# Loading the first batch's queries and keys in whole rows, and turning them one head at a time

## The chip, the cores and the metric

The program runs on one core of a Trainium2 chip. The metric is device time in microseconds (us) of one execution. TensorE (PE) does the matrix products, VectorE (DVE), ScalarE (ACT) and GpSimd (POOL) the elementwise work, and SyncE (SP) issues every transfer between memory and the core. Sixteen DMA engines carry the transfers out.

## The reference, cut to what matters

Windowed attention over 4 batches, 8 heads, 576 tokens and a head size of 64, then a two-layer MLP, then a gated MLP. All inputs are float32 or wider.

```
scores = q @ k.T / sqrt(64)          # heads 0-3: window of 32; heads 4-7: every 4th of the last 128
attn   = softmax(where(mask, scores, -1e9))
x  = attn @ v                        # as 2304 tokens x 512
x2 = leaky_relu(x @ w_in) @ w_out    # 512 -> 2048 -> 512
y  = ((x2 @ w1) * (x2 @ w2)) @ w3 @ w_out2
```

## The kernel before, in words

**Heads.** Two heads make a pair, so a pair of a batch fills the 128 rows of the PE array with 2 x 64. A batch has four pairs: two with the dilated mask, which come first, and two with the plain one. `seq` is the order of the pairs, and the number m in `load_qk(m)` and `transpose_qk(m)` counts q and k through it. So m = 0 to 7 is the first batch (`m < 2 * HP`).

**Loading q and k** (`load_qk`, issue at L244). For a pair with c = 8 (dilated) or 6 (plain), each of n = 576 / c partitions holds c consecutive tokens: 72 or 96 partitions. In the tile, the token comes before the head, so that one token's two heads lie side by side:

```
t = win_p.tile([P, 8, 2, D], F32, tag="win", ...)
nc.sync.dma_start(t[:n, :c, j, :], rows(src, o + j * S * D, [[c * D, n], [D, c], [1, D]]))
```

There is one transfer for each head j. It writes runs of 64 floats (256 bytes), 576 of them.

**Turning q and k round** (`transpose_qk`, L306). For each of c token positions, one PE transpose takes n x 128 (both heads) to 128 x n in a PSUM bank; DVE copies half a tile at a time to `qT` (L309, with the scale) or `kT` (L311). The scores of a pair (L328) follow, then mask and maximum on DVE (L336, L338), exponentials on ACT (L341), the turn of the probabilities (L371, L373), and the values (L389, L420, L422).

**Weights.** The inputs of both MLPs are 64-bit floats. A `conv.fetch()` issues one raw weight tile of 512 KB (L127 for w_in, L124 for w_out, in turn); a `conv.step()` converts one tile with POOL (L103), ACT (L143, L145, L107) and DVE (L146, L147, L108) and fetches the next. There are 32 tiles for the first MLP. Eight can be fetched before one is converted.

**Order.** SP's instructions keep the order in which the program writes them; the other engines are ordered by a planner that estimates times and takes what is ready, in the program's order of importance. The order at the start is one string. A digit loads q and k of a pair of the first batch, a letter a to d loads values (`load_v`, L282), M builds the masks, F fetches a weight tile, X starts the attention, A does two of its steps, C converts a weight tile:

```
for x in "0aM1bFF2cFF3dFFFFXAAAAAAAAAAAACCCCCCCC":
```

The weight tiles that these F fetch are called F0 to F7 here, and the four pairs by their digits. After this start the hidden layer (L112 to L114 into `ps_h`) and its projection (`ps_x`) run on PE, with the attention of later batches woven in.

Of the kernel before, what the change touches and what calls it, by code (L numbers as in the profile page):

```python
# [8 lines left out]
F32 = mybir.dt.float32  # L9
# [19 lines left out]
def tile_window_attention_two_mlps(  # L29
# [14 lines left out]
    nc = tc.nc  # L44
    P = 128
    B, H, S, D = q.shape
# [5 lines left out]
    NF = F1 // P  # L52
# [12 lines left out]
    HP = H // 2  # L65


    def pool(name, side):
        es = ExitStack()
        return es, es.enter_context(  # L70
            tc.tile_pool(name=name, bufs=1, side=side, reuse_waits="tile")
        )
# [3 lines left out]
    win_es, win_p = pool("win", "left")  # L76
# [17 lines left out]
    ident = const.tile([P, P], F32, name="ident")  # L94
# [24 lines left out]
    def rows(t, off, dims):  # L119
        return bass.AP(t.tensor, t.offset + off, dims)  # L120
# [67 lines left out]
    win, wout, w12, wo2, wp = {}, {}, {}, {}, {}  # L188
# [37 lines left out]
    def pair(pi):  # L226
        b, h0 = divmod(pi, HP)
        return b, 2 * h0, 2 * h0 < H // 2

    def load_qk(m):  # L230
        if m >= 2 * NPAIR:
            return
        pi, nm = seq[m // 2], "qk"[m % 2]
        b, h0, plain = pair(pi)
        c = 6 if plain else 8
        n = S // c
        if m < 2 * HP:
            t = win_p.tile([P, 8, 2, D], F32, tag="win", name=f"{nm}{pi}", bufs=NF)
        else:
            t = att.tile([P, 8, 2, D], F32, tag="nat", name=f"{nm}{pi}", bufs=2)  # L240
        src = q if nm == "q" else k
        o = (b * H + h0) * S * D
        for j in range(2):
            nc.sync.dma_start(  # L244
                t[:n, :c, j, :], rows(src, o + j * S * D, [[c * D, n], [D, c], [1, D]])
            )
        nat_t[nm, pi] = t


# [8 lines left out]
    def load_v(m):  # L258


        if m >= 4 * B:
            return
        b, plain, r = m // 4, m % 4 >= 2, m % 2
        o = (b * H + (0 if plain else H // 2)) * S * D
        bl = R_BLOCKS[r]
        tiles = []
        if m >= 4:
            t = att.tile([KB, NQ, H // 2, D], F32, tag="v", name=f"v{m}", bufs=2)
            tiles = [t[:, i] for i in range(len(bl))]
        else:  # L270
            for i0 in range(0, len(bl), 4):
                t = win_p.tile([KB, 4, H // 2, D], F32, tag="win", name=f"v{m}_{i0}", bufs=NF)
                tiles += [t[:, i] for i in range(min(4, len(bl) - i0))]
        for i, t in zip(bl, tiles):
            k0 = s0 = first_key(i, plain)
            while s0 < k0 + KB:
                if plain:
                    s1, token, st = k0 + KB, s0, D
                else:
                    s1 = min(k0 + KB, (s0 // SR + 1) * SR)  # L280
                    token, st = s0 % SR * DILATION + s0 // SR, DILATION * D
                nc.sync.dma_start(  # L282
                    t[s0 - k0 : s1 - k0], rows(v, o + token * D, [[st, s1 - s0], [S * D, H // 2], [1, D]])
                )
                s0 = s1
        v_t[m] = tiles

    def transpose_qk(m):

        if m >= 2 * NPAIR:  # L290
            return
        pi, nm = seq[m // 2], "qk"[m % 2]
        plain = pair(pi)[2]
        c = 6 if plain else 8
        n = S // c
        t = nat_t.pop((nm, pi))
        dst = att.tile([P, S], F32, tag=nm + "T", name=f"{nm}T{pi}", bufs=2)
        if plain:
            to = dst.rearrange("d (p g c) -> d g c p", g=2, p=n)
        else:  # L300
            to = dst.rearrange("d (c p g) -> d g c p", g=2, p=n)
        for g in range(2):
            ps = (bank if m < 2 * HP else side_bank)(f"ps_{nm}T{pi}_{g}")
            for c1 in range(c // 2):
                src = t[:n, g * (c // 2) + c1].rearrange("p j d -> p (j d)")
                nc.tensor.transpose(ps[:, c1 * n : (c1 + 1) * n], src, ident[:n, :n])  # L306
            src = ps[:, : S // 2].rearrange("d (c p) -> d c p", p=n)
            if nm == "q":
                nc.vector.tensor_scalar(to[:, g], src, SCALE, None, op0=ALU.mult)  # L309
            else:  # L310
                nc.vector.tensor_copy(to[:, g], src)  # L311
        qk_t[nm, pi] = dst
# [116 lines left out]
    def attention(n0, n1):  # L429

        for n in range(n0, n1):
            if n == N_EARLY:
                for m in range(NA, NA + 2):
                    load_qk(m)
                load_v(4)
                for m in range(NA, n + 4):
                    transpose_qk(m)
                    load_qk(m + 2)
                load_v(5)
            transpose_p(n)  # L440
            normalize(n + 1)
            yield
            if n % 8 != 3:
                scores(n + 2)
                yield
            if n >= N_EARLY or n + 4 < NA:
                transpose_qk(n + 4)
            if n >= N_EARLY:
                load_qk(n + 6)
            yield  # L450
            if n % 8 == 3:
                scores(n + 2)
                yield
            values(n)
            if n >= NA:
                m = n // NA * 4
                if n % NA in (2, 3):
                    load_v(m + n % NA)
                elif n % NA in (5, 7):
                    load_v(m + 4 + (n % NA == 7))  # L460
            yield
# [178 lines left out]
    with ExitStack():  # L640
# [5 lines left out]
        def build_masks():  # L646


            def band(m, shift):
                for j in range(2):  # L650
                    mj = m[j * QB : (j + 1) * QB]
                    for base, sign in ((shift, 1), (WINDOW - 1 - shift, -1)):
                        nc.gpsimd.affine_select(
                            out=mj, in_=mj, compare_op=ALU.is_ge, fill=NEG, base=base,
                            pattern=[[-sign, KB]], channel_multiplier=sign,
                        )

            shifts = [i * QB - first_key(i, False) for i in range(S // QB)]
            band(mask_d[:, 0], shifts[0])
            band(mask_d[:, 1], WINDOW)  # L660
            nc.vector.tensor_copy(mask_p[:, 0], mask_d[:, 0])
            for m in (mask_d[:, 2:], mask_p[:, 1:]):
                nc.vector.tensor_copy(m, mask_d[:, 1:2].to_broadcast(list(m.shape)))
            for i in range(2, S // QB):
                if shifts[i] != WINDOW:
                    nc.vector.memset(mask_d[:, i], 0.0)
                    band(mask_d[:, i], shifts[i])

                x = ((i * QB) // SR + 1) * SR - first_key(i, False)
                if x < KB:  # L670
                    for j in range(2):
                        mj = mask_d[j * QB : (j + 1) * QB, i, :x]
                        nc.gpsimd.affine_select(
                            out=mj, in_=mj, compare_op=ALU.is_ge, fill=NEG, base=x - shifts[i] - 1,
                            pattern=[[0, x]], channel_multiplier=-1,
                        )
# [20 lines left out]
        with tc.manual_schedule(engines={mybir.EngineType.SP}):  # L697


            first = attention(0, N_EARLY)  # L700
            for x in "0aM1bFF2cFF3dFFFFXAAAAAAAAAAAACCCCCCCC":
                if x in "0123":
                    load_qk(2 * int(x))
                    load_qk(2 * int(x) + 1)
                elif x in "abcd":
                    load_v("abcd".index(x))
                elif x == "M":
                    build_masks()
                elif x == "X":
                    transpose_qk(0)  # L710
                    transpose_qk(1)
                    scores(0)
                    scores(1)
                    transpose_qk(2)
                    normalize(0)
                    transpose_qk(3)
                elif x == "A":
                    step(first, first)
                elif x == "F":
                    conv.fetch()  # L720
                else:
                    conv.step()
            step(*[first] * 10)
# [169 lines left out]
```

## Time and profile before

| | |
|---|---|
| median of 3 runs | 917.64 us (916.98 to 919.58) |
| the profiled execution | 918.02 us, of which the span from first to last instruction is 916.2 us |
| PE busy | 880.8 us (96%) |
| DVE, ACT, POOL busy | 345.9, 354.5, 247.8 us |
| mean granted PE clock | 0.974 of full speed |

An engine's busy time is the time in which at least one of its instructions runs. Times in rows are microseconds from the first instruction. In brackets behind a row stands how long the engine was idle before it, and what ended that idle time. SPq is SP's queue: its rows are the issuing of transfers, not the transfers.

### The profile page before, as it was taken

How to read it: one execution, taken by the hardware profiler on the slowest of the kernel's cores; microseconds unless marked ns; L12 is line 12 of the kernel's file. 1: busy time of each engine (PE TensorE's matmuls, PEld its weight loads, DVE VectorE, ACT ScalarE, POOL GpSimd, SP SyncE). 2: the span in 40 equal slices, each digit the busy share in tenths (PEclk: the TensorE clock that was granted, in tenths of full speed). 3: DMA queues.
4: the chain of work that ended last, by engine and by line, in shares of the span. 5: the costliest groups of instructions: out<-in, count | busy, mean ns of one | idle time of the engine just before them, and what ended most of it. 6: DMA issues, size and time to landing. Idle time of an engine off the chain costs nothing.

```text
span 916.2 us, 16026 instructions
## 1 busy us (share of the span) xinstructions
PE 880.8 (96%) x6456; PEld 832.4 (91%) x6456; DVE 345.9 (38%) x699; ACT 354.5 (39%) x904; POOL 247.8 (27%) x288
## 2 busy tenths in 40 slices
PE   4869899999999999999999999999999999999998
PEld 4658799999999999999999999999999998999997
DVE  4999864444333233264334345851101010100000
ACT  3898742433333333365333245742212121211211
POOL 3454410012222223254222143432213031211110
PEclk9559999999999999999999999999999999999999
DMA  7995502322213102177788665620101010000000
GB/s 170 313 271 129 180 19 57 83 48 73 49 44 78 45 14 62 47 252 282 235 293 271 211 201 160 202 79 1 46 24 35 35 35 24 12 24 12 12 24 35
DMA packets 110938, 95.94 MB, mean 105 GB/s; under 512 B 69520, under 2 KB 94352, under 8 KB 110864
## 3 DMA queue, kind: packets, MB, share of 16 engines
q1 hardware_dynamic: 110864, 94.92, 34.8%
q8 instruction: 51, 0.84, 0.4%
q14 instruction: 23, 0.19, 0.1%
HBM read 78.51 MB, written 16.38 MB: 104 GB/s over the span
## 4 chain that ended last, share of the span: by engine, by line
PE 82%; DVE 6%; ACT 3%; DMA 3%; SPq 2%; issue 2%; POOL 1%; DVEq 0%; POOLq 0%; ACTq 0%
PE ps_ab L112 7%; PE ps_ab L114 7%; PE ps_ab L113 7%; PE ps_h L113 6%; PE ps_h L114 6%; PE ps_x L112 6%; PE ps_h L112 6%; PE ps_x L114 6%; PE ps_x L113 6%; PE ps_y L113 4%; PE ps_y L112 4%; PE ps_y L114 4%; PE ps_s L328 2%; PE ps_o L389 2%; PE ps_wp L114 2%
## 5 line engine op out<-in xcount | busy, mean ns | idle before, releaser
L112 PE MATMUL ps_h<-x,win 128*128 128x320 f32 (+1 forms) x512 | 154.7, 303 | 3.6 <-DMA v<-in_v_dram 2.3
L113 PE MATMUL ps_h<-x,win 128*128 128x320 f32 (+1 forms) x512 | 155.4, 304 | 1.1 <-DVE x L422 1.1
L113 PE MATMUL ps_x<-gs,wout 128*128 128x320 f32 (+1 forms) x512 | 152.8, 299 | 2.4 <-DVE gs L108 2.4
L114 PE MATMUL ps_h<-x,win 128*128 128x320 f32 (+1 forms) x512 | 154.4, 302 | 0.0
L112 PE MATMUL ps_x<-gs,wout 128*128 128x320 f32 (+1 forms) x512 | 152.1, 299 | 1.1 <-DVE x L509 1.1
L114 PE MATMUL ps_x<-gs,wout 128*128 128x320 f32 (+1 forms) x512 | 152.7, 299 | 0.0
L112 PE MATMUL ps_ab<-ys,w 128*128 128x384 f32 x384 | 130.1, 339 | 0.0
L114 PE MATMUL ps_ab<-ys,w 128*128 128x384 f32 x384 | 130.0, 339 | 0.0
L113 PE MATMUL ps_ab<-ys,w 128*128 128x384 f32 x384 | 130.0, 338 | 0.0
L616 DVE TENSOR_TENSOR ab<-a,ps_ab 128x384 f32<-128x384 f32 x48 | 26.6, 554 | 253.0 <-ACT a L614 247.9
L107 DVE CAST gs<-g 128x320 fp32r<-128x320 f32 (+1 forms) x128 | 49.7, 391 | 153.6 <-ACT g L473 153.4
L108 POOL TENSOR_TENSOR p<-ab,p 128x384 fp32r<-128x384 f32 x48 | 48.5, 1011 | 218.6 <-ACT p L107 218.6
L108 POOL TENSOR_TENSOR gs<-g,gs 128x320 fp32r<-128x320 f32 (+1 forms) x80 | 66.4, 831 | 145.2 <-DVE gs L107 145.2
L112 PEld LDWEIGHTS ps_h<-x,win 128*128 128x128 f32 x512 | 97.9, 192 | 5.3 <-ACT x L420 4.2
L113 PEld LDWEIGHTS ps_x<-gs,wout 128*128 128x128 f32 x512 | 96.9, 189 | 3.8 <-DVE gs L108 2.9
L113 PEld LDWEIGHTS ps_h<-x,win 128*128 128x128 f32 x512 | 98.3, 192 | 2.1 <-DVE x L422 1.3
L112 PEld LDWEIGHTS ps_x<-gs,wout 128*128 128x128 f32 x512 | 96.5, 189 | 2.6 <-DVE x L509 1.3
L114 PEld LDWEIGHTS ps_h<-x,win 128*128 128x128 f32 x512 | 98.4, 192 | 0.3
L114 PEld LDWEIGHTS ps_x<-gs,wout 128*128 128x128 f32 x512 | 96.9, 189 | 0.5
L473 ACT ACTIVATE g<-ps_h 128x320 f32<-128x320 f32 (+1 forms) x128 | 51.4, 403 | 115.2 <-PE ps_h L114 114.1
L614 ACT COPY a<-ps_ab 128x384 f32<-128x384 f32 x48 | 23.0, 480 | 143.9 <-PE ps_ab L114 143.9
L112 PEld LDWEIGHTS ps_ab<-ys,w 128*128 128x128 f32 x384 | 72.0, 188 | 1.2
(91 smaller groups left out, 1514.8 us busy)
## 6 DMA issues: line engine op xcount, KB each, us to landing
wo<-wo_dram SPq DMA_DIRECT2D x32, 512.0 KB
raw<-in_moe_w_in_dram SPq DMA_DIRECT2D x16, 512.0 KB
raw<-in_moe_w_out_dram SPq DMA_DIRECT2D x16, 512.0 KB
rawf<-in_moe_w_dram SPq DMA_DIRECT2D x16, 512.0 KB
raww<-in_moe_w_dram SPq DMA_DIRECT2D x16, 512.0 KB
v<-in_v_dram SPq DMA_DIRECT2D x60, 96.0 KB
q<-in_q_dram SPq DMA_DIRECT2D x32, 144.0 KB
k<-in_k_dram SPq DMA_DIRECT2D x32, 144.0 KB
```

Of the source, the lines that this page charges most:

```text
L107: copy_on(e_hi)(hi, src)
L108: e_lo.tensor_tensor(lo, src, hi.bitcast(F32), op=ALU.subtract)
L112: nc.tensor.matmul(ps, a[1], b[0], start=first, stop=False)
L113: nc.tensor.matmul(ps, a[0], b[1], start=False, stop=False)
L114: nc.tensor.matmul(ps, a[0], b[0], start=False, stop=last)
L328: nc.tensor.matmul(ps[j * QB : (j + 1) * QB, i - bl.start], qt[d, i * QB : (i + 1) * QB], kt[d, first_key(i, plain) : first_key(i, plain) ...
L389: nc.tensor.matmul(ps[j * D : (j + 1) * D, i * QB : (i + 1) * QB], vt[i][:, h + j, :], t[:, i, j * QB : (j + 1) * QB], start=True, stop=True,)
L473: nc.scalar.activation(g, ps, AF.Prelu, alpha=SLOPE)
L614: nc.scalar.copy(t, ps[0][:, :TB])
L616: nc.vector.tensor_tensor(g, t, ps[1][:, :TB], op=ALU.mult)
```

## The change

For the first batch, the tile has the head before the token, so each partition's tokens of one head are one run in the tile, as they are in memory: 2,048 bytes for 8 tokens, 1,536 for 6. The two heads of a token then no longer lie side by side, and the turn is made for one head at a time: a product of the n x 64 slice with the identity into half of the PSUM rows, twice as many instructions as the transposes before. Later batches keep the old layout and the transposes. In the string, F1 moves behind the loads of pair 2 and of values c, and F2 and F3 move behind those of pair 3 and of values d.

```
-            t = win_p.tile([P, 8, 2, D], F32, tag="win", name=f"{nm}{pi}", bufs=NF)
+            t = win_p.tile([P, 2, 8, D], F32, tag="win", name=f"{nm}{pi}", bufs=NF)
...
-            nc.sync.dma_start(
-                t[:n, :c, j, :], rows(src, o + j * S * D, [[c * D, n], [D, c], [1, D]])
-            )
+            to = t[:n, j, :c, :] if m < 2 * HP else t[:n, :c, j, :]
+            nc.sync.dma_start(to, rows(src, o + j * S * D, [[c * D, n], [D, c], [1, D]]))
...
-                src = t[:n, g * (c // 2) + c1].rearrange("p j d -> p (j d)")
-                nc.tensor.transpose(ps[:, c1 * n : (c1 + 1) * n], src, ident[:n, :n])
+                cols = slice(c1 * n, (c1 + 1) * n)
+                if m < 2 * HP:
+                    for j in range(2):
+                        nc.tensor.matmul(
+                            ps[j * D : (j + 1) * D, cols], t[:n, j, g * (c // 2) + c1],
+                            ident[:n, :n], start=True, stop=True,
+                        )
+                else:
+                    src = t[:n, g * (c // 2) + c1].rearrange("p j d -> p (j d)")
+                    nc.tensor.transpose(ps[:, cols], src, ident[:n, :n])
...
-            for x in "0aM1bFF2cFF3dFFFFXAAAAAAAAAAAACCCCCCCC":
+            for x in "0aM1bF2cF3dFFFFFFXAAAAAAAAAAAACCCCCCCC":
```

## Rows read from the trace of the kernel before

**Rows 1.** The page's first part: busy time, share of the span, instructions.

```profile
PE 880.8 (96%) x6456; PEld 832.4 (91%) x6456; DVE 345.9 (38%) x699; ACT 354.5 (39%) x904; POOL 247.8 (27%) x288
```

**Rows 2.** Stages of 20 us: length, busy by engine (instructions), clock, DMA share, GB/s.

```profile
0.00:20.00 20.00, 10.51 (x97) 8.87 (x97) 8.50 (x22) 5.59 (x21) 7.72 (x27) 0.91 0.70 170
20.00:40.00 20.00, 15.02 (x133) 11.68 (x135) 17.10 (x36) 17.00 (x56) 7.64 (x8) 0.58 1.05 277
40.00:60.00 20.00, 12.10 (x122) 9.54 (x118) 18.38 (x38) 19.73 (x56) 10.41 (x12) 0.59 1.01 289
60.00:80.00 20.00, 17.45 (x115) 16.26 (x116) 19.85 (x33) 16.05 (x30) 9.61 (x10) 0.81 0.97 248
80.00:100.00 20.00, 18.35 (x151) 17.00 (x151) 18.93 (x36) 15.23 (x39) 8.80 (x9) 1.00 0.26 81
100.00:120.00 20.00, 16.74 (x152) 15.13 (x151) 17.22 (x38) 17.98 (x46) 8.65 (x9) 0.91 0.56 168
120.00:140.00 20.00, 20.00 (x189) 19.50 (x188) 9.39 (x24) 6.16 (x22) 2.61 (x2) 1.00 0.07 16
...
400.00:420.00 20.00, 18.89 (x144) 18.34 (x143) 13.66 (x21) 11.87 (x22) 11.63 (x13) 1.00 0.92 317
```

**Rows 3.** SP's queue in order of time: start, length, line, transfer, how many.

```profile
0.74 1.85 SPq L244 DMA_DIRECT2D q<-in_q_dram  x2
2.63 1.63 SPq L244 DMA_DIRECT2D k<-in_k_dram  x2
4.30 3.95 SPq L282 DMA_DIRECT2D v<-in_v_dram  x7
...
14.30 0.48 SPq L127 DMA_DIRECT2D raw<-in_moe_w_in_dram  x1
14.84 0.49 SPq L124 DMA_DIRECT2D raw<-in_moe_w_out_dram  x1
...
23.20 0.49 SPq L127 DMA_DIRECT2D raw<-in_moe_w_in_dram  x1
```

**Rows 4.** Single instructions of PE, ACT and DVE in order of time.

```profile
5.41 1.19 PE L306 MATMUL ps_qT<-ident,q 72*128 72x72 f32 x8 [5.41 <-DMA q<-in_q_dram]
...
19.03 0.79 ACT L143 ACTIVATE r<-raw 128x512 f16<-128x512 f32 x1 [2.84 <-DMA raw<-in_moe_w_in_dram]
...
19.77 0.43 DVE L146 TENSOR_SCALAR w<-w 128x512 int32<-128x512 int32 x1 [2.71 <-POOL w L103]
...
21.40 0.78 ACT L143 ACTIVATE r<-raw 128x512 f16<-128x512 f32 x1 [0.96 <-DMA raw<-in_moe_w_out_dram]
...
22.34 0.69 PE L306 MATMUL ps_qT<-ident,q 96*128 96x96 f32 x6 [2.77 <-DMA q<-in_q_dram]
...
27.65 0.80 ACT L143 ACTIVATE r<-raw 128x512 f16<-128x512 f32 x1 [0.24 <-DMA raw<-in_moe_w_in_dram]
```

**Rows 5.** The DMA queue, 10 to 15 us and 36 to 50 us: packets, MB, share.

```profile
q1 hardware_dynamic: 3532, 0.88, 79.3%
...
q1 hardware_dynamic: 3621, 5.23, 106.2%
```

**Rows 6.** PE in order of time: turns of q and k, and values products.

```profile
14.62 0.70 PE L306 MATMUL ps_kT<-ident,k 72*128 72x72 f32 x8 [0.90 <-DMA k<-in_k_dram]
...
26.52 1.22 PE L306 MATMUL ps_kT<-ident,k 96*128 96x96 f32 x6
...
29.23 1.12 PE L389 MATMUL ps_o<-pT,v 96*64 96x64 f32 x16
...
87.33 0.69 PE L389 MATMUL ps_o<-pT,v 96*64 96x64 f32 x16
```

**Rows 7.** Shorter stages, columns as in group 2.

```profile
10.00:15.00 5.00, 3.77 (x48) 3.39 (x45) 3.25 (x7) 2.15 (x12) 0.00 (x0) 1.00 0.79 175
...
25.00:30.00 5.00, 4.82 (x44) 3.75 (x43) 4.09 (x9) 4.58 (x13) 2.68 (x3) 0.50 1.12 294
...
60.00:67.00 7.00, 5.76 (x24) 5.47 (x25) 6.85 (x10) 5.51 (x10) 4.76 (x5) 0.50 0.90 264
```

## The prediction

> **What bounds the kernel now.** I read the page's busy times first: PE is busy for 880.8 us, 96% of the span [rows 1], so at most 35 us can be idle. The table by stages says where they lie. From 120 us on PE is busy without a gap (the row of 120 to 140 us stands for nearly all that follow), but for two short gaps (one is in the row of 400 to 420 us, which lacks 1.1 us); the first 120 us lack almost 30 [rows 2]. In these, DVE is the full engine from 20 us on: 91.5 of 100 us, with ACT at 17.0 and 19.7 of 20 between 20 and 60 us. Before 20 us it is busy for only 8.5 [rows 2]. So the start has two parts: some 20 us that wait for data, then 100 us of attention and weight conversion that DVE and ACT pace. Behind 120 us PE's work is fixed. Time saved in the first part moves everything behind it, if the second part has nothing new to wait for.
>
> The waits of the first part are in the order of time. PE's first turn waits for q until 5.41 us. ACT and DVE wait for F0 until 19.03 and 19.77 us (2.84 and 2.71 us idle), ACT again for F1 until 21.40 us (0.96 us), PE for pair 2's q until 22.34 us (2.77 us), ACT a little for F2 until 27.65 us [rows 4]. What makes these late is SP's queue. It issues without a pause from 0.74 us: four loads of q and k take 3.5 us, seven of v 3.95, and F0 is issued at 14.30 us, F2 at 23.20 [rows 3]. The DMA engines are not full until then: 0.70 over the first 20 us, 0.97 to 1.05 over the next 60 [rows 2].
>
> **The change, part by part.**
>
> *Issue of the loads.* A load of q or k holds SP for 1.63 / 2 = 0.82 us; a load of v, whose destination rows are unbroken, for 3.95 / 7 = 0.56 with the gaps, a weight tile for 0.49 [rows 3]. The new load has an unbroken run on both sides, so the nearest row is the weight tile's: 0.49, a saving of 0.33. If the issue cost follows the partitions and not the runs, the saving is nothing; that is the other bound. I take 0.33. Eight such loads stand ahead of F0, so F0 is issued 8 x 0.33 = 2.6 us earlier, at 11.7 us.
>
> *Transfer.* From 10 to 15 us nearly all packets are 256-byte runs: 0.88 MB take 0.793 x 16 x 5 = 63.4 engine-us, 13.9 KB per us and engine. Weight tiles move 5.23 MB in 1.062 x 16 x 14 = 238 engine-us, 22.0 KB [rows 5]. The first batch's q and k are 16 loads of 147 KB, 2.36 MB: 10.6 us on 16 engines at the first rate, 6.7 at the second. That frees 3.9 us of DMA time, half of it ahead of F0. What F0 gets of it: it arrived 19.03 - 14.78 = 4.25 us after its issue ended, while the first two loads of q, on an empty queue, needed 5.41 - 2.59 = 2.8 us [rows 3, 4]. A tile of 512 KB adds 0.524 / 0.352 = 1.5 us at 16 x 22.0 KB, less the 0.7 that a small load itself took: 3.6 us. So F0 comes at 11.7 + 0.5 + 3.6 = 15.8 us, 3.2 earlier; the bounds are 0 (both terms fail) and 4.
>
> *Start of the attention.* q and k of pair 0 are issued in 2.0 us, not 3.5, and move at the faster rate, so the first scores come 1.5 to 2 us earlier. The masks that DVE and POOL build at the start are not touched.
>
> *The moved fetches.* F1 goes behind four loads of q and k (4 x 0.49) and five of v (5 x 0.56): issue at 12.2 + 2.0 + 2.8 = 17.0 us, where it was 14.84 [rows 3]. With 0.5 + 3.6 it comes at 21.1, against 21.40 before [rows 4]: no gain. F2 goes behind four more and four of v: 17.5 + 2.0 + 2.2 = 21.7, against 23.20 [rows 3], and comes near 26 us, 1.5 to 2 earlier than 27.65 [rows 4]. F4 to F7 need no longer wait for pair 3. In return q of pair 2 is issued at 12.2 us and comes at 15 to 16, some 6 us before its turn at 22.34 [rows 4], and pair 3's loads go out from 17.5 us on, where they stood behind F2 and F3, at 23.20 + 2 x 0.5 = 24.2. So at 16 us DVE and ACT have F0, at 21 us F1, and between them attention that before was not there. SP's is the only queue passed; POOL issues nothing here. If the attention between them is too little, the cover is gone and F1 is late next (rival B).
>
> *Products for transposes.* The eight tiles had 4 x 8 + 4 x 6 = 56 transposes; they become 112 products. The trace shows the very form in the values products (96 rows by 64 columns, output in alternating halves of the banks): 16 in 0.69 us at full clock (the stage of 80 to 100 us), 43 ns each for 64 moving columns, and 16 in 1.12 us at half clock, 70 ns [rows 2, 6, 7]. For 72 columns that is 49 ns, and a dilated tile's 16 take 0.78 us where its 8 transposes took 0.70 (clock 1.00). For 96 columns at half clock it is 105 ns, 12 take 1.26 where 6 took 1.22 [rows 6, 7]. Together 4 x 0.08 + 4 x 0.04 = 0.5 us, in a stretch where PE is idle for 40 - 10.5 - 15.0 = 14.5 us [rows 2]: nothing. If two halves didn't overlap, each tile would take twice as long, 4 x 0.70 + 4 x 1.22 = 7.7 us, of which pair 0's 1.4 would delay the first scores and nearly eat that gain.
>
> The Trainium skill speaks against this part: *Perfetto Trace Analysis*, section Transposes, asks for the transpose operation and not a standard matmul, and *TensorE: Matmul & The Clock Gate*, section Terms, calls transpose mode four times faster for float32. By that rule the tiles would take 23 us more; by the rows above they take 0.5.
>
> *Sum.* DVE's and ACT's full stretch begins as much earlier as F0, 3.2 us, less 0.2 for the products of pairs 0 and 1: 3.0. Of this DVE can use it, as it has 11.5 idle us before 20. Against the profiled execution: 918.02 - 3.0 = 915.0; the median lies 0.4 lower, so **914.6 us**.
>
> **Rivals.**
>
> *A, the forecast:* 914.6, by itself 913.0 to 916.1, as F0's gain comes out between 1.5 and 4.6 with the rest of the attention's. Chance 0.50.
>
> *B, given back at F1:* DVE and ACT work in the planner's order. If F1's conversion stands where it did, right behind F0's, the wait of 2.71 us moves from F0 to F1, which comes only 0.3 us earlier. For it: F1 is issued 2.2 us later. Against: in the string all attention steps are ahead of the conversions, so attention that is ready should go first. If the loads' issue doesn't get shorter, it also ends here. 0 to 1.2 us gained: 917.0. Chance 0.22.
>
> *C, more than the shift:* between 60 and 67 us the first hidden layer runs at a clock of 0.50 and PE is busy for 5.76 us [rows 7]. If the attention ahead of it closes up, since pair 2's and 3's data lie ready, the clock has risen by then, and the same products take half: 2.9 us more, 911.7. For it: the DMA wait at 22.34 us goes. Against: DVE, which paces that attention, is full anyway. Chance 0.18.
>
> *D, slower:* the products are ordinary float32 ones and cost four times a transpose, with their halves overlapping. That adds 3 x 0.70 = 2.1 us per dilated tile at full clock and 3 x 1.22 = 3.7 per plain one, 23.2 in all, against 14.5 idle on PE until 40 us. 8.7 stay, less the 3.0: 923. It decides from (14.5 + 5.5) / 112, about 0.18 us for a product, on: there PE becomes the first bound of the start. For it: only a rule; the rows of the same form show 0.05 to 0.105. The Trainium skill's two sections named above are that rule. That the planner's new order turns out worse somewhere later is in this chance too. Chance 0.10.
>
> **How the numbers follow.** The measurement tells 0.3%, 2.75 us: below 914.9 is faster, above 920.4 slower. A reaches below 914.9 with 0.30 of its 0.50, C wholly: 0.48 faster. The rest of A and B: 0.42 the same. D: 0.10 slower. The range is 911.0 to 918.0: it takes in A, B and most of C, and leaves out D and C's far end, 0.15 together. A's own is 913.0 to 916.1.
>
> **What would show it.** In the profile after: SP's rows at L244 for the first batch at about 0.5 us each, F0 issued near 11.7 us and converted from 16 us; the packets of the first 15 us in larger runs and few of them; 16 (or 12) products of L306 in 0.8 us (1.3 at half clock); the first scores before 8 us; DVE busier than 8.5 us before 20 us; and PE full from 117 us on. The forecast is wrong if the issue stays at 0.8 us, if a wait for F1 of 3 us stands on DVE, if the products take over 0.1 us at full clock, or if DVE's stretch gets as much longer as it begins earlier.

## The result, and the profile after

The changed kernel takes 922.66 us (median of 6 runs, 921.35 to 927.69), the kernel before 917.80 beside it: ratio 1.0059, interval 1.0033 to 1.0085. It is slower, by 0.6%. The forecast was 914.6 us, in a range from 911.0 to 918.0.

In the changed kernel's numbering the first batch's q and k are loaded at L245, v at L281, the products are L307, the transposes that remain L313, `qT` and `kT` L316 and L318, scores L335, mask addition L343, exponentials L348, values L396, and the attention's result `x` L429 (L422 before).

The page's first part, and the table by stages (columns as in group 2):

```profile
PE 885.5 (96%) x6624; PEld 837.8 (91%) x6624; DVE 342.8 (37%) x699; ACT 354.5 (39%) x904; POOL 248.5 (27%) x288
```

```profile
0.00:20.00 20.00, 12.56 (x164) 11.37 (x164) 7.80 (x20) 6.10 (x22) 6.65 (x26) 0.96 0.79 194
20.00:40.00 20.00, 16.11 (x188) 13.00 (x187) 16.81 (x36) 15.81 (x46) 9.48 (x11) 0.67 1.09 352
40.00:60.00 20.00, 11.90 (x137) 9.82 (x135) 18.62 (x38) 19.34 (x53) 9.11 (x10) 0.50 0.90 238
60.00:80.00 20.00, 13.42 (x90) 11.70 (x91) 18.22 (x34) 17.85 (x45) 12.10 (x13) 0.67 0.75 211
80.00:100.00 20.00, 20.00 (x187) 19.07 (x185) 18.39 (x41) 15.97 (x42) 6.71 (x8) 1.00 0.26 79
100.00:120.00 20.00, 18.30 (x156) 17.26 (x153) 19.23 (x33) 16.51 (x39) 9.58 (x10) 1.00 0.38 129
```

PE's busy time rose by 885.5 - 880.8 = 4.7 us [rows 1], and the span by 920.1 - 916.2 = 3.9: its idle time hardly changed. DVE, which was to start earlier, is busy for 7.80 us of the first 20, less than the 8.50 of before. Between 60 and 80 us PE does 4 us less than before (13.42 against 17.45), at a lower mean granted clock (0.67 against 0.81) [rows 2]; there the hidden layer, begun at 61.5 us, stood for turns and for attention (PE's rows, in order of time, of the changed kernel and then one of the kernel before):

```profile
67.96 0.74 PE L313 MATMUL ps_qT<-ident,q 72*128 72x72 f32 x4 [2.37 <-DVE qT L316]
...
73.50 0.64 PE L113 MATMUL ps_h<-x,win 128*128 128x320 f32 x1 [1.31 <-DVE x L429]
73.92 0.47 PE L114 MATMUL ps_h<-x,win 128*128 128x320 f32 x1
```

```profile
62.61 0.63 PE L113 MATMUL ps_h<-x,win 128*128 128x320 f32 x1 [1.08 <-DVE x L422]
```

SP's queue (columns as in group 3) issued in the forecast's order and near its times:

```profile
0.74 0.81 SPq L245 DMA_DIRECT2D q<-in_q_dram  x2
1.59 0.78 SPq L245 DMA_DIRECT2D k<-in_k_dram  x2
2.42 3.78 SPq L281 DMA_DIRECT2D v<-in_v_dram  x7
...
10.49 0.48 SPq L127 DMA_DIRECT2D raw<-in_moe_w_in_dram  x1
...
17.62 0.48 SPq L124 DMA_DIRECT2D raw<-in_moe_w_out_dram  x1
...
22.48 0.39 SPq L127 DMA_DIRECT2D raw<-in_moe_w_in_dram  x1
```

The first loads hold SP for 0.81 / 2 = 0.41 us, where it was 0.82 [rows 3]. F0 is issued at 10.49 us (forecast 11.7), F1 at 17.62 (17.0), F2 at 22.48 (21.7). Next, single instructions of PE, ACT and DVE in order of time:

```profile
3.55 2.47 PE L307 MATMUL ps_qT<-ident,q 72*64 72x72 f32 x31 [3.55 <-POOL masks L660]
...
8.95 1.67 PE L307 MATMUL ps_qT<-ident,q 72*64 72x72 f32 x16 [0.47 <-DMA q<-in_q_dram]
10.55 3.14 PE L335 MATMUL ps_s<-kT,qT 64*64 64x96 f32 x36
...
18.87 1.23 PE L307 MATMUL ps_kT<-ident,k 72*64 72x72 f32 x16 [3.35 <-DVE qT L316]
```

```profile
16.74 0.78 ACT L143 ACTIVATE r<-raw 128x512 f16<-128x512 f32 x1 [0.93 <-DMA raw<-in_moe_w_in_dram]
...
27.38 0.80 ACT L143 ACTIVATE r<-raw 128x512 f16<-128x512 f32 x1 [2.04 <-DMA raw<-in_moe_w_in_dram]
```

```profile
12.53 0.66 DVE L343 TENSOR_TENSOR s<-ps_s,masks 128x480 f32<-128x480 f32 x1 [1.42 <-PE ps_s L335]
...
17.56 0.43 DVE L146 TENSOR_SCALAR w<-w 128x512 int32<-128x512 int32 x1 [3.19 <-POOL w L103]
...
22.91 0.43 DVE L146 TENSOR_SCALAR w<-w 128x512 int32<-128x512 int32 x1 [1.34 <-POOL w L103]
```

F0 is converted on ACT from 16.74 us, 2.3 earlier than the 19.03 of before [rows 4]. PE's first turn starts 1.9 us earlier, at 3.55 against 5.41 [rows 4], and yet the first scores come only at 10.55 us, where they came at 9.49 before:

```profile
9.49 3.15 PE L328 MATMUL ps_s<-kT,qT 64*64 64x96 f32 x36 [0.55 <-DVE kT L311]
```

The products of pair 0 hold PE until about 8.5 us, and in the new order the first turn of pair 1 (the row of 8.95 us) stands ahead of the scores too. The row of 18.87 us shows an attention turn that waited for DVE, and DVE's row of 17.56 us is the conversion that stood in front of it, itself 3.19 us late for F0.

The products first. The program issues 112; the trace has 224 records of them, two each. All turns of the first batch, changed kernel and then the kernel before, as stages of L307 and L306 alone (busy time of PE and of weight loads):

```profile
0.00:60.00 60.00, 18.48 (x224) 15.31 (x224) 0.71 0.92 262
```

```profile
0.00:50.00 50.00, 8.45 (x56) 6.51 (x56) 0.70 0.91 253
```

So the turns cost 10.0 us more of PE, and a product took 18.48 / 112 = 0.165 us, where a transpose took 8.45 / 56 = 0.151.

What came after 40 us is a matter of order. Markers of both traces, from the rows of DVE and PE in order of time (a conversion is counted by its DVE instruction, L147):

| | before | changed |
|---|---|---|
| mask addition of the eighth scores | 52.8 us | 60.9 us |
| conversions ahead of it on DVE | 9 | 14 |
| first product of the hidden layer | 51.0 us | 61.5 us |
| first product of its projection | 70.4 us | 80.6 us |
| 16th conversion | 70.0 us | 69.1 us |

The planner drew a new order. Conversions keep their pace (the 16th comes as before), attention is 8 us later, and the hidden layer that needs it 10 us later.

### The profile page after: what moved, and what is told of

It reads as the page before. It is cut to its first block, busy times and chain, and to the rows that moved or that the text cites. A ratio compares the mean times of both kernels' runs of the same rounds, so it can differ in the third digit from the quotient of the medians.

```text
span 920.1 us, 16348 instructions
## 1 busy us (share of the span) xinstructions
PE 885.5 (96%) x6624; PEld 837.8 (91%) x6624; DVE 342.8 (37%) x699; ACT 354.5 (39%) x904; POOL 248.5 (27%) x288
## 4 chain that ended last, share of the span: by engine, by line
PE 81%; DVE 6%; DMA 5%; ACT 4%; issue 2%; POOL 1%; SPq 1%; DVEq 0%; ACTq 0%; POOLq 0%
PE ps_ab L112 7%; PE ps_ab L114 7%; PE ps_ab L113 7%; PE ps_x L112 6%; PE ps_x L114 6%; PE ps_x L113 6%; PE ps_h L113 6%; PE ps_h L114 6%; PE ps_h L112 6%; PE ps_y L113 4%; PE ps_y L112 4%; PE ps_y L114 4%; PE ps_s L335 2%; PE ps_o L396 2%; PE ps_wp L114 2%
```

## Experiments

Each time is set against the kernel before on the same chip (917 to 918 us), as a ratio with its 95% interval. The expectations name theories by letters. P: the products are the loss. F: the moved fetches are. N: each edit draws another order, and nothing adds up. O: the planner's new order is the loss. F1 (in the last group): with an order held fixed, the string costs what DVE or ACT waits for F1. "Scores 7" counts from 0 and is the eighth.

### Parts of the change, each under the planner's own order

**x1**, the string alone.

```
-            for x in "0aM1bFF2cFF3dFFFFXAAAAAAAAAAAACCCCCCCC":
+            for x in "0aM1bF2cF3dFFFFFFXAAAAAAAAAAAACCCCCCCC":
```

> The kernel before with the new string alone: old loads, old transposes. Theory P (the products are the loss: PE spends 18.5 us on the eight turns where it spent 8.45): no loss from the string, 0 +- 1.5 us against before. Theory F (the moved fetches are the loss: the planner puts the conversion of F0 ahead of the attention, so that DVE waits 3 us with the attention queued behind it): +3 to +5 us. Theory N (each change of the start only draws another order from the planner, with no cause that adds up): anywhere within +-5.

**x2**, layout and products, with the old string.

```
-            t = win_p.tile([P, 8, 2, D], F32, tag="win", name=f"{nm}{pi}", bufs=NF)
+            t = win_p.tile([P, 2, 8, D], F32, tag="win", name=f"{nm}{pi}", bufs=NF)
...
+                            ps[j * D : (j + 1) * D, cols], t[:n, j, g * (c // 2) + c1],
+                            ident[:n, :n], start=True, stop=True,
```

> Rows and products with the old string. Theory P: as slow as the changed kernel, +4 to +6 us against before. Theory F: the loss is gone, 0 to -3 us. Theory N: anything.

**x3**, the new layout with transposes, as many as before. Each takes two tokens of one head in place of one token of both heads, so the first batch's q and k reach the scores with heads and tokens mixed; the work and its shapes are the same.

```
+                if m < 2 * HP:
+                    src = t[:n, g, 2 * c1 : 2 * c1 + 2]
+                    nc.tensor.transpose(ps[:, cols], src.rearrange("p j d -> p (j d)"), ident[:n, :n])
```

> Loads in whole rows, the old string, and the old transposes. A transpose then takes two tokens of one head instead of one token of two heads, so q and k get mixed values; number, shape and length of all instructions are those of before. It prices the loads alone. Theory P: the forecast's gain without the products' price, -2 to -4 us. Theory F: also -2 to -4. If the loads' gain was an error of the forecast: 0 +- 1.5.

**x4**, the products alone, on the old layout, loads and string.

```
+                    for j in range(2):
+                        nc.tensor.matmul(
+                            ps[j * D : (j + 1) * D, c1 * n : (c1 + 1) * n],
+                            t[:n, g * (c // 2) + c1, j], ident[:n, :n], start=True, stop=True,
+                        )
```

> The kernel before with products, one head at a time, in place of the first batch's transposes; old loads, old string. It prices the products alone. Theory P: +5 to +9 us (10 us more of PE time in the start, most of it on the chain of the attention, and the rows' gain is missing). Theory F: 0 +- 1.5, since PE has 14.5 idle us in the first 40.

| | us | ratio | conversions ahead of the eighth scores |
|---|---|---|---|
| x1 string | 916.20 | 0.9978 [0.9968, 0.9989] | 8 |
| x2 rows and products | 923.96 | 1.0060 [1.0046, 1.0075] | 15 |
| x3 rows and transposes | 906.77 | 0.9876 [0.9861, 0.9891] | 9 |
| x4 products | 916.62 | 0.9983 [0.9973, 0.9992] | 9 |

The whole loss is there in x2, without the string, as theory P says. But P wanted 5 to 9 us of loss from x4, and the products alone made the kernel 1.6 us faster; and x3, from which P and F both wanted a gain of 2 to 4 us, gained 11. x2 and x3 differ by 17.2 us, while PE's time in their turns differs by 8.4 (17.44 against 9.04). Sizes of parts alone don't explain this. The last column says what else moves: each edit gets another order.

### The start written by hand

**h1, h2, h3**: the kernel before, with rows and products, and with rows and transposes (mixed as in x3), DVE, ACT and POOL kept in program order at the start, and one string for all three.

```
-        with tc.manual_schedule(engines={mybir.EngineType.SP}):
+        hand = {mybir.EngineType.SP, mybir.EngineType.DVE, mybir.EngineType.Activation, mybir.EngineType.Pool}
+        with tc.manual_schedule(engines=hand):
...
+            for x in "0aM1bFF2cFF3dFFFFXCAACAACCAAAACCCAACCAACCCCCCCC":
```

> The kernel before with the start's instructions of DVE, ACT and POOL in an order written out by hand: attention first, with 1, 2, 4, 4, 7 and 9 conversions ahead of the mask additions of scores 2 to 7, close to the planner's own order of before (0, 2, 3, 6, 8, 9). It is the base for the two runs beside it. Both theories: within 5 us of before.

> Rows and products (the changed kernel's, old string) in the same order by hand; the first 100 instructions of DVE and the first 70 of ACT stand in the same order as in the base. Theory O (the loss is the planner's order: it puts 14 conversions ahead of scores 7, where before had 9, and the attention that the hidden layer waits for comes 11 us later): the loss is gone, -4 to +1 us against the base by hand. Theory P (the products' PE time of 8 to 10 us itself): +4 to +8 against the base by hand.

> Rows and transposes (two tokens of one head, so that values are mixed) in the same order by hand. Theory O: within 3 us of the run with products, -1 to -5 against the base. Theory P: 8 us or more faster than the run with products.

Measured: h1 933.58 (1.0177 [1.0157, 1.0197]), h2 937.26 (1.0214 [1.0198, 1.0230]) and h3 930.16 (1.0135 [1.0117, 1.0153]). The hand-made order is bad by itself: h1 was expected within 5 us of before and is 16 slower. Within it rows save 3.4 us and products add 7.1 on top of them, nearer to theory P than to O.

**h4**, the changed kernel with every weight fetch behind all loads of the first batch, planner's order.

```
-            for x in "0aM1bF2cF3dFFFFFFXAAAAAAAAAAAACCCCCCCC":
+            for x in "0aM1b2c3dFFFFFFFFXAAAAAAAAAAAACCCCCCCC":
```

> The changed kernel, order by the planner, with all eight fetches behind the loads of q, k and v. The planner then puts 10 conversions ahead of scores 7, not 14. Theory O: faster than the changed kernel although every weight comes later, 914 to 919. Theory P: no faster than the changed kernel, 922 or more, as the products are all there and F0 comes 8 us later.

Measured: 918.42, 1.0009 [0.9998, 1.0019], 4 us better than the changed kernel although F0 itself is issued later; the first conversion on DVE comes at 27.1 us, not 19.0. Ten conversions stand ahead of the eighth scores. That is within theory O's range, and an early F0 alone is not what the time hangs on.

### One kernel's instructions in another kernel's order

Here the whole planned order of DVE, ACT, POOL and PE of one kernel is laid on the instructions of another: each instruction gets an ordering edge to the one ahead of it on its engine. The products of one turn take the place of its transpose.

```
+                for k in seq[:upto.get(eng, len(seq))]:
+                    for i in units[k]:
+                        if prev is not None:
+                            tc.add_manual_dep(i, prev.name, info, reason="order")
+                        prev = i
```

> The changed kernel (rows, products, new string), but DVE, ACT, POOL and PE keep, from the first instruction to the last, the order that the planner gave the kernel before; a pair of products stands in the place of its transpose. Theory O (the planner's order is the loss): the loss is gone, 914 to 918 us. Theory P (the products themselves, +7, against the rows' gain of 3.4, as under the order by hand): the loss stays, 920 to 923. Both by halves would give 918 to 920.

> The kernel before (strided loads, transposes, old string) in the order that the planner gave the changed kernel, on the same four engines. Theory O: as slow as the changed kernel or slower, 921 to 927, since attention waits behind 14 conversions here too. Theory P: faster than the changed kernel by the products' price less the rows' gain, 918 to 920.

> The kernel before in the order that the planner gave the run with rows and transposes (906.8 us). If that run's 11 us are its order's and the rows give 3.4 as under the order by hand: 909 to 911. If they are the rows' own: 916 to 919.

> The changed kernel in that same order. Theory P: the products' price on top of 906.8, 912 to 915. Theory O: within 3 us of that run, 906 to 910. A version that beats both kernels by either.

**v1**, a control: the changed kernel with its own order laid on by the same edges.

> The changed kernel, with the planner's own order for DVE, ACT, POOL and PE imposed by the same ordering edges that carried the orders of other kernels. If the edges themselves cost nothing, it repeats the changed kernel: 922 to 923 us, ratio 1.004 to 1.007. If they cost something, it is slower by that, and the four kernels in imposed orders have to be read with it.

| instructions of | in the order of before | of the changed kernel | of x3 |
|---|---|---|---|
| before | 1 (as it is) | s2: 924.73, 1.0082 [1.0070, 1.0094] | s3: 911.79, 0.9938 [0.9927, 0.9950] |
| changed | s1: 920.86, 1.0035 [1.0023, 1.0047] | v1: 921.57, 1.0047 [1.0034, 1.0059] | s4: 914.60, 0.9968 [0.9955, 0.9981] |

The edges cost nothing that can be told (v1 against 1.0059). Read along a row, the order alone moves the changed kernel by (1.0047 - 0.9968) x 918 = 7.3 us and the kernel before by 13.2. Read down a column, the new instructions cost 3.2 us in the order of before and 2.8 in x3's, and save 3.2 in the order that was planned for them. So O's expectation held for s2 (the kernel before becomes as slow), and P's for s1 and s4 (the loss stays in a better order): both are at work. s3, the kernel before in x3's order, is 0.6% faster than the kernel before, and s4 also beats both.

### The parts in the order of before

With the order of before laid on, an edit's own size can be read: **r1** rows and products, **r2** rows and transposes (mixed as in x3), **r3** products on the old loads, **r4** the string. Their edits are those of x2, x3, x4 and x1 with the edges added. The edges add lines to kernel.py: in the rows below L133, L136 and L152 are the lines that are L124, L127 and L143 in the other kernels, L317 is the turn of the first batch, L324 and L327 are the changed kernel's L313 and L316, and L346 is its L335.

> Rows and products, the old string, in the order of before. Theory P: +2 to +4 us against before. Theory F1: the wait for F1 is gone, 0 to -4.

> Rows with transposes (two tokens of one head, so that values are mixed), the old string, in the order of before. Both theories: the loads' gain alone, -3 to -5 us against before, as by hand (-3.4) and in the order of x3 (-5.0). If the rows' gain depends on the order: -1 to +1.

> The old loads with products, the old string, in the order of before. Theory P: +5 to +8 us against before. Theory F1: +1 to +3.

> The kernel before with the new string alone, in its own old order. Theory F1: F1 comes later by its place in SP's queue and DVE waits for it, +3 to +5 us against before. Theory P: 0 +- 1.

| | us | ratio | against before |
|---|---|---|---|
| r2 rows | 914.76 | 0.9967 [0.9956, 0.9979] | -3.0 |
| r3 products | 919.88 | 1.0025 [1.0013, 1.0036] | +2.3 |
| r1 rows and products | 917.28 | 0.9995 [0.9984, 1.0006] | -0.5 |
| r4 string | 924.13 | 1.0068 [1.0051, 1.0086] | +6.2 |
| s1 all three | 920.86 | 1.0035 [1.0023, 1.0047] | +3.2 |

Rows and products add up (-3.0 + 2.3 = -0.7, measured -0.5). r1 and r3 lie where theory F1 expected them, and P's price of 5 to 8 us for r3 did not come. The string costs 3.7 us on top of them, 6.2 alone, which is more than F1's 3 to 5. What waits for it stands in r4's ACT rows, in order of time:

```profile
19.27 0.79 ACT L152 ACTIVATE r<-raw 128x512 f16<-128x512 f32 x1 [3.02 <-DMA raw<-in_moe_w_in_dram]
27.57 0.78 ACT L152 ACTIVATE r<-raw 128x512 f16<-128x512 f32 x1 [6.89 <-DMA raw<-in_moe_w_out_dram]
```

In an order that takes F1 right behind F0, ACT waits 6.89 us for F1, until 27.57; it was 0.96, until 21.40 [rows 4]. s1 has the same wait, a little shorter (SP's row, then ACT's). The profiled executions of r4 and s1 took 926.32 and 925.83 us, the longest of each.

```profile
18.91 0.48 SPq L133 DMA_DIRECT2D raw<-in_moe_w_out_dram  x1
```

```profile
25.92 0.78 ACT L152 ACTIVATE r<-raw 128x512 f16<-128x512 f32 x1 [6.46 <-DMA raw<-in_moe_w_out_dram]
```

And r2's rows show the forecast's term by itself, F0 on SP and then on ACT:

```profile
10.36 0.48 SPq L136 DMA_DIRECT2D raw<-in_moe_w_in_dram  x1
```

```profile
15.48 0.80 ACT L152 ACTIVATE r<-raw 128x512 f16<-128x512 f32 x1 [1.43 <-DMA raw<-in_moe_w_in_dram]
17.86 0.79 ACT L152 ACTIVATE r<-raw 128x512 f16<-128x512 f32 x1 [0.97 <-DMA raw<-in_moe_w_out_dram]
```

F0 is converted 3.55 us earlier than before, F1 as much, and 3.0 us of it reach the end.

The first scores come before 8 us, as was forecast, in r2 alone (7.33); with the products they come at 8.76 in r1, still earlier than before (PE's rows of r1, the first scores and then the 16 products that turn pair 1's q):

```profile
8.76 3.15 PE L346 MATMUL ps_s<-kT,qT 64*64 64x96 f32 x36 [0.55 <-DVE kT L329]
...
11.84 1.58 PE L317 MATMUL ps_qT<-ident,q 72*64 72x72 f32 x32
```

### Is it the conversions ahead of the attention?

**v2**: v1 with one group moved. All instructions of conversions 9 to 16 that stood ahead of the eighth attention step follow it: 18 on DVE, 17 on ACT, 9 on POOL. On DVE, from the sixth scores on (w is a step of a conversion, with its number):

```
-s5 w10 nmax5 wout w11 w12 x x win s6 w13 total5 nmax6 rec5 w12 w13 s7 x nmax7
-w14 total6 w15 win rec6 w14 wout w16 qT total7 rec7 qT
+s5 nmax5 x x s6 total5 nmax6 rec5 s7 x nmax7 total6 rec6 qT total7 rec7
+w9 w9 w10 w11 w10 wout w11 w12 win w13 w12 w13 w14 w15 win w14 wout w16 qT
```

> The same, with one group moved: every instruction of weight conversions 9 to 16 that stood ahead of the eighth attention step on DVE, ACT and POOL (18, 17 and 9 instructions) follows it. Everything else keeps its order. If the changed kernel is slow because its order puts 14 conversions ahead of that attention and so delays the first hidden layer, this gains 3 to 6 us on the imposed order without the move: 917 to 920, with the sixth attention done on DVE near 65 us, not 73. If the loss lies elsewhere (the products, F1's wait), it stays within 1 us of it. If the conversions were needed early, it is slower, since the hidden layer then waits for weights.

Measured: 929.17, 1.0122 [1.0107, 1.0138], 7.6 us slower than v1. The eighth mask addition did come earlier, 57.2 us against 61.7, but not the sixth attention step (80.9 us against 73.7). PE's rows, in order of time:

```profile
61.36 0.47 PE L324 MATMUL ps_qT<-ident,q 72*128 72x72 f32 x4 [0.17 <-DVE qT L327]
77.16 0.74 PE L324 MATMUL ps_kT<-ident,k 72*128 72x72 f32 x4 [15.32 <-DVE qT L327]
```

PE stands for 15.32 us before a turn of the second batch, whose `qT` copy on DVE now stood behind all the moved conversions. So the gain that was expected did not come, and the run doesn't decide on the conversions: the move put something else behind them. (The expectation's last clause, slower because the hidden layer waits for weights, is not what happened either.) That 14 conversions ahead of the attention are the order's loss is not shown.

But v2 points at the sixth attention step: it came 7.2 us later, and the kernel took 7.6 us more. With that step the attention of the first 320 tokens is complete, and the hidden layer's long run on PE waits for it (PE's rows of 73.50 and 62.61 us in the section on the result). Its write of `x` on DVE, changed kernel and then the kernel before:

```profile
72.96 0.48 DVE L429 TENSOR_TENSOR x<-ps_o,x 128x320 fp32r<-128x320 f32 x1
```

```profile
62.08 0.48 DVE L422 TENSOR_TENSOR x<-ps_o,x 128x320 fp32r<-128x320 f32 x1
```

| | that write at | us |
|---|---|---|
| x3 rows and transposes | 55.87 | 906.77 |
| r2 rows, order of before | 58.37 | 914.76 |
| r1 rows and products, order of before | 59.81 | 917.28 |
| s3 before, order of x3 | 60.77 | 911.79 |
| s4 changed, order of x3 | 61.23 | 914.60 |
| before | 62.08 | 917.80 |
| r3 products, order of before | 62.34 | 919.88 |
| x1 string | 62.40 | 916.20 |
| x4 products | 63.33 | 916.62 |
| h4 fetches last | 65.37 | 918.42 |
| s1 changed, order of before | 66.39 | 920.86 |
| r4 string, order of before | 68.07 | 924.13 |
| changed | 72.96 | 922.66 |
| v1 changed, own order | 73.72 | 921.57 |
| x2 rows and products | 75.53 | 923.96 |
| s2 before, order of the changed kernel | 77.69 | 924.73 |
| v2 | 80.88 | 929.17 |

The first column is from the profiled execution, the second the median. Left out are the three by hand, which lose time elsewhere too (h3: 63.77 and 930.16). In the main, the later that step, the longer the kernel, whatever put it there, but with a scatter of some 5 us, and not us for us: from before to changed the step moves by 10.9 us and the kernel by 4.9. It is a pattern over runs, not an experiment on that step alone.

## Why the prediction was wrong

**What bounds the kernel** was read rightly as far as the trace goes: PE waits in the first 120 us and is full behind them.

**Issue and transfer of the loads: the sum came out, its terms did not.** The issue saved more than was forecast: 0.41 us a load in place of 0.33, and F0 was issued at 10.36 us in r2 and 10.49 in the changed kernel, not at 11.7. The transfer saved nothing: F0 was to come 3.6 us after its issue ended, and came 15.48 - 10.84 = 4.6 us after it in r2 and 16.74 - 10.97 = 5.8 in the changed kernel, where it had been 4.25. The forecast took this term from a load on an empty queue, but from 10 to 15 us the DMA engines were now busy for 0.98 of the time, against 0.79 before [rows 5]; r2's row:

```profile
q1 hardware_dynamic: 2169, 1.36, 97.8%
```

That the fuller engines are why F0 took longer is likely, and no run separates it. The two misses nearly cancel in r2, where F0 came 3.55 us earlier (forecast 3.2); that is partly luck. In the changed kernel it came 2.3 us earlier. By itself this part saves 3.0 us at the end in the old order (r2).

**Products for transposes, "nothing": the first step that failed.** The forecast took 16 rows of the values line for 16 products. The trace writes each float32 product as two records, so they were 8, and every price was half of what it should have been. Doubled, the forecast's 49 ns for 72 columns are 0.098 us, and r1's 16 products of pair 1 took 1.58 us, 0.099 each, at a granted clock of 1.00; its 105 ns for 96 columns at half clock are 0.21, and the changed kernel's take 1.23 us for 12 records, 0.205 for a product (from 34.41 us on, clock 0.50). For pair 0, 16 transposes took 2.39 us before and the 32 products 4.86 after (stages of all PE work; nothing else runs on PE there):

```profile
5.00:9.00 4.00, 2.39 (x16) 2.02 (x16) 1.42 (x5) 0.00 (x0) 2.25 (x10) 1.00 0.77 170
```

```profile
3.50:8.50 5.00, 4.86 (x64) 4.46 (x64) 2.06 (x7) 0.00 (x0) 2.50 (x11) 1.00 0.83 197
```

So the turn of a pair takes twice as long. (Both stages show a clock of 1.00, but 8 transposes take 1.19 us there [rows 4], against 0.70 for pair 1's k at the same 1.00 [rows 6]: the two stages can be set against each other, but their lengths are not those of full speed.) The forecast's clause for tiles that take twice as long was near: 7.7 us for all tiles and 1.4 on pair 0, which "would delay the first scores and nearly eat that gain". Its reason was halves that don't overlap, and whether they do no run here tells. Measured are 10.0 us more on PE in the changed kernel, 4.2 in the order of before (14.15 in r1 against 9.92 in r2).

The price was not all that failed. At the doubled prices the forecast's working gives 16 x 0.098 - 0.70 = 0.87 us more for a dilated tile and 12 x 0.21 - 1.22 = 1.30 for a plain one, 8.7 in all: less than PE's 14.5 idle us, and so by its own test still nothing. But 2.5 us of r1's 4.2 reach the end (r1 against r2), and 2.3 on the old loads (r3): PE's idle time did not take it all up. The first scores, which wait for pair 0's turns, come 1.4 us later in r1 than in r2.

The factor of four that the Trainium skill gives (*TensorE: Matmul & The Clock Gate*, section Terms) is not what these rows show: a product took 0.165 us where a transpose took 0.151, and 18.48 / 8.45 = 2.2 for the whole comes from two products in place of one transpose. Its advice against such products (*Perfetto Trace Analysis*, section Transposes) was the right side to be on here.

**The moved fetches, "no gain": right only with an order that fills the wait.** F1 was issued at 17.62 us, near the forecast's 17.0, but here too the 3.6 us failed: in s1 F1 came 25.92 - 18.91 - 0.48 = 6.5 us after its issue ended. In the order of before this costs 3.7 us on top of the rest: rival B's mechanism, at more than its price. In the planner's own order the wait is mostly filled (DVE waits 1.34 us at 22.91, ACT 2.04 for F2 at 27.38), and there the string costs nothing: x2, without it, is as slow as the changed kernel.

**The sum: the second step that failed.** It let DVE's and ACT's full stretch begin earlier and go on as before. It does not go on as before: the planner sorts it anew. The same changed instructions take 1.0047 in that order and 0.9968 in x3's. With transposes in place of the products, on the same loads and string (x3 against x2), it put 9 conversions ahead of the eighth scores and not 15, and the sixth attention step came at 55.9 us and not at 75.5. Rival D named this in its last clause. That its 923 was met within 0.4 us is luck: it was worked out from a product at four transposes, which is not what was measured, and its bound of 0.18 us for a product was not reached (0.165); the 5.5 us in that bound come from no row it names.

**The account.** In the order of before, set against the forecast's -3.0: -3.0 for the rows, +2.5 for the products on them, +3.7 for the string, together +3.2 us. The planner's own order adds 1.1 to that by v1 (2.2 by the first timing), within what the intervals can tell. Along the planner's orders it reads otherwise: rows and products +5.5 (x2), where they were -0.5 in the old order, and the string nothing. The sizes themselves go with the order: products cost 7.1 us by hand (h2 against h3), and in x3's order rows save 5.7 (x3 against s3) and products and string together cost 8.4 (s4 against x3). All of these are measured, and the parts don't add across orders, so no single share can be given to the string or to the order. Which instructions of the new order cost the time stays open. What is seen is that the sixth attention step comes late there, and conversions ahead of attention; moving those (v2) made that step later still.

**Rival C** did not happen: the first records of the hidden layer's long run still take 0.47 us each, in the changed kernel from 74 us on as before from 63, and 0.31 only from 77 us on (69 before). The clock rose 3 us after that run began, where it was 6 before, but 8 us later in the kernel.

## What to carry to other kernels

Where a planner orders the engines, an edit is two edits: its own instructions, and the order that the planner draws from them. Lay one kernel's order on the other's instructions before judging either; here the order was worth up to 13 us and the whole edit 3, and the fastest kernel that keeps q and k unmixed was the old one in another's order (s3). Before a price per instruction is read from a trace, divide the records by what the program issues: a record is not always an instruction. And that an engine is idle for longer than the extra work does not make the work free: look for what waits for it.

## What the runs showed that was not expected

Each float32 product with the identity leaves two records on PE, while each transpose leaves one: 112 products are 224 records in 18.48 us, 56 transposes 56 in 8.45. A load that writes one run of 2 KB for each of 72 partitions holds SP's queue for 0.41 us at the start, half of the 0.82 of one that writes 576 runs of 256 bytes [rows 3]; right behind F0, pair 2's q held it for 0.83 us a load all the same.
